# Weight conversion as a pipeline over units, and x's parts spread over the seven products, in an attention + MoE kernel

## The chip, the cores and the metric

The kernel runs on one core of a Trainium2 chip. The metric is the device time of one execution in microseconds; the comparison is between medians of several executions. The engines are named as the profile names them: PE (matmuls; PEld its weight loads), DVE (vector), ACT (scalar), POOL (GpSimd) and SP, which issues every DMA of this kernel. Each of them works through its own instructions strictly in the order of the program; instructions of different engines wait for each other by semaphores. A "DMA" is issued by SP and done by 16 shared transfer engines.

## The reference

Causal attention with a decay over 8 x 8 heads (576 positions, 64 dimensions each), and behind it a two-layer network on the 4608 tokens of 512 features. The second part is the one that the change touches:

```python
def _moe_ref(x, w_in, w_out) -> np.ndarray:
    h = x @ w_in                                   # 4608x512 @ 512x2048
    sp = np.maximum(h, 0.0) + np.log1p(np.exp(-np.abs(h)))
    g = h * erf(sp)
    return (g @ w_out).astype(np.float32)          # 4608x2048 @ 2048x512
```

The two weight matrices arrive as 64-bit floats, so the kernel has to make 32-bit floats of them itself.

## The kernel before, in words

**Two phases.** For the first 335 us the core does attention, head by head, and beside it begins to convert weights. Then comes the network ("Moe" in the code), which is all that the change moves.

**How the network is tiled.** The 4608 tokens are six blocks of 768 (`PAIR`), and the 2048 hidden features are eight units of 256. Half of the units (four, `HU`) are worked through for all six blocks, then the other half: twelve *visits* v = 0 to 11, each of four units k = 0 to 3. A *step* n = 4v + k is one unit of one visit; there are 48. Visits 0 to 5 are the first half (steps 0 to 23), visits 6 to 11 the second. A visit's partial output goes to DRAM in the first half (`part_d`) and is read back and added in the second. "A boundary" is the change from one visit to the next, step k = 3 into step k = 0.

**A step on PE.** The first product (`product`, line 149) multiplies 2x2 blocks with seven instead of eight block products; i = 0 to 6 is such a product. Every operand is carried as two parts, a rounded one and the remainder, so that each product is six matmuls of 384 columns (two along the features times three pairs of parts). x therefore stands as seven combinations, numbered r = 0 to 6, each with a rounded part and a remainder; the products use them in the order 0, 5, 1, 4, 6, 2, 3 (`XSLOT`). Only two PSUM banks (m) serve the seven products; `consume` takes a product out of its bank before a later product writes the bank again: copies `sa` and `h` on ACT (lines 162 and 167), sums `sb`, `sc` and `h` on DVE (lines 165, 170 and 173). Between the products stand the 36 matmuls of the second product (`down`, line 210, into the banks y) of the unit of two steps before; `YCUT` says after which product how many of them stand.

**Beside it, for the unit of the step before.** Four softplus and four erf on ACT (lines 177 and 180), four multiplications on DVE ("gates", line 183), four rounded copies `gh` on ACT (line 192) and four remainders `gl` on POOL (line 193), which are what `down` multiplies ("halves"). Softplus and erf need different tables in ACT: two table loads a step, at line 180 and, called for ahead of time, at line 274.

**x's parts.** `load_x` fetches the four blocks t0 to t3 of the next visit, issued at the start of k = 2. `x_sum` makes two combinations on POOL (lines 108 and 110), `late_sum` two on DVE (line 131, in place, t0 then t1); `split_x` is the rounded copy on ACT (line 117) and `rest_x` the remainder (line 123), on DVE for r = 0 and 5 and on POOL for the rest. The parts of the next visit are made in k = 3, and part 3 at the very start of its k = 0, because each part takes the place of the one that the products of k = 3 still read.

**Weight conversion.** A *piece* is 512 KB of 64-bit weights (`raw`); there are 22 in the network phase. `load` issues its DMA; `magnitude` takes the absolute value on ACT (line 372, |x|, which is in the table that erf uses and not in softplus's); `normal`, `low_bits` (two instructions) and `join` (lines 375 to 388) put a 32-bit float together on DVE; `parts` makes the rounded part on ACT (line 399) and the remainder on POOL (line 400), and for units of the second half stores both to DRAM (`wi_d`, `wo_d`; lines 402 and 403). A piece of `w_in` has one to six such pairs of parts, one of `w_out` a single one, used directly in `wo` for the first half. In the network phase all these are kept in one list, and `filler` takes the next one to three of them from it after each product, by the table `FILL`. There is one raw buffer, and the next piece is loaded at the end of `join`.

**What sets the order.** Everything is written out by hand: the program's order on each engine is the order of the calls in `step`.

## Time and profile before

| | |
|---|---|
| three runs | 1211.41, 1214.77 and 1215.17 us, median 1214.77 |
| the profiled execution | 1212.26 us, its span 1210.5 us, mean granted clock 0.967 |
| busy in the span | PE 92%, ACT 67%, DVE 59%, POOL 55% |
| attention, to step 2 | 0 to 350.7 us |
| steps 3 to 21 (conversion beside the network) | 366.8 to 767.2 us |
| steps 22 to 47 | 767.2 to 1186.5 us |
| a step that PE fills | 15.75 us |

A row of a view by stretches names the stretch in us, its length, then each engine's busy time and instructions, the granted clock of PE as a share of full speed, the DMA engines' busy share and GB/s. A row of groups has line, engine, operation, output and inputs, count, then busy us, mean ns, and the engine's idle time ahead of such instructions with what ended it. A row of waits reads "engine line <- what ended the wait: us in total, times, longest". A row of the timeline is start, duration, engine, line, operation, count and, in brackets, idle time ahead of it. A busy PE is not a PE at its peak: the half-rate clock makes it busy for longer.

### The profile page before, as it was taken

Reading aid. Unit: us, or ns where it says so; the run is one execution under the profiler, and the core shown is the slowest. Engines: PE = TensorE matmul, PEld = TensorE weight load, DVE = VectorE, ACT = ScalarE, POOL = GpSimd, SP = SyncE. Lnnn points to the kernel's source line nnn. Section 1 sums busy time; section 2 is a strip of 40 time slices with the busy share of each in tenths; the row PEclk is TensorE's granted clock in tenths of the full one; section 3 lists DMA queues with packets and bytes.
Section 4 is the critical chain, followed back from the end, with each engine's and each line's share of the span. In section 5 each row is a group of like instructions: output and inputs, shape, how many; then the busy total and the mean of one; then the engine's idle time right before and its main releaser. Section 6 shows DMA issues by size and latency. Waiting matters only on the chain. (4 is left out here: it accounts for less than half of the span.)

```text
span 1210.5 us, 21366 instructions
## 1 busy us (share of the span) xinstructions
PE 1115.7 (92%) x7384; PEld 968.0 (80%) x7384; DVE 708.3 (59%) x1696; ACT 813.2 (67%) x1746; POOL 666.6 (55%) x808
## 2 busy tenths in 40 slices
PE   8999999999997678888797989999999999999997
PEld 7888878878886567776686877989888888989896
DVE  6899989998646554555656454353444444444432
ACT  5878878878765567576767786566756656666652
POOL 5787878888815525635456436363526263553522
PEclk9999999999998798898998999999999999999999
DMA  7778777866221123251161331535040312203021
GB/s 252 239 232 262 221 234 237 290 215 201 73 90 35 53 99 119 70 170 65 61 209 35 118 135 61 214 143 209 1 156 1 111 46 68 89 28 131 9 96 70
DMA packets 74908, 155.83 MB, mean 129 GB/s; under 512 B 7472, under 2 KB 27184, under 8 KB 73776
## 3 DMA queue, kind: packets, MB, share of 16 engines
q1 hardware_dynamic: 74800, 154.47, 38.3%
q8 instruction: 59, 0.97, 0.3%
q14 instruction: 49, 0.40, 0.1%
HBM read 114.44 MB, written 39.99 MB: 128 GB/s over the span
## 5 line engine op out<-in xcount | busy, mean ns | idle before, releaser
L149 PE MATMUL m<-x,wi 128*128 128x384 f32 x2016 | 427.5, 348 | 55.6 <-DVE h L173 28.5
L149 PEld LDWEIGHTS m<-x,wi 128*128 128x128 f32 x2016 | 375.0, 194 | 95.9 <-ACT sa L162 31.8
L193 POOL TENSOR_TENSOR gl<-e,gh 128x384 fp32r<-128x384 f32 x192 | 213.3, 1142 | 393.2 <-ACT gh L192 368.4
L210 PE MATMUL y<-wo,gh 128*128 128x512 f32 x1152 | 384.0, 401 | 21.4 <-ACT wo L399 18.9
L210 PEld LDWEIGHTS y<-wo,gh 128*128 128x128 f32 x1152 | 219.5, 192 | 56.7 <-ACT wo L399 20.2
L210 PE MATMUL y<-wo,gl 128*128 128x512 f32 x576 | 231.4, 402 | 0.0
L578 POOL TENSOR_SCALAR pr<-pr,st 128x576 f32<-128x576 f32 (+4 forms) x320 | 165.1, 538 | 49.6 <-DVE st L574 29.6
L568 ACT ACTIVATE pr<-pr,st 128x576 f32<-128x576 f32 (+3 forms) x320 | 176.7, 557 | 5.0 <-DVE st L556 5.0
L556 DVE CUSTOM_DVE_ANT_0 pr<-s,c 128x576 f32<-128x576 f32 (+3 forms) x320 | 136.5, 486 | 25.5 <-PE s L540 18.2
L177 ACT ACTIVATE e<-h 128x384 f32<-128x384 f32 x192 | 92.3, 519 | 55.9 <-DVE h L173 53.3
L183 DVE TENSOR_TENSOR e<-e,h 128x384 f32<-128x384 f32 x192 | 95.4, 559 | 56.3 <-ACT e L180 56.1
L210 PEld LDWEIGHTS y<-wo,gl 128*128 128x128 f32 x576 | 111.2, 193 | 17.6
L536 PE MATMUL s<-k,q 64*128 64x320 f32 (+4 forms) x768 | 109.9, 407 | 1.9 <-DVE st L556 1.9
L599 ACT COPY pt<-t 128x512 f32<-128x512 f32 x128 | 74.0, 578 | 55.7 <-PE t L590 53.9
L165 DVE TENSOR_TENSOR sb<-m,sa 128x384 f32<-128x384 f32 x48 | 26.7, 557 | 143.8 <-PE m L149 88.5
L123 POOL TENSOR_TENSOR x<-t,x 128x768 fp32r<-128x768 f32 x55 | 108.5, 2003 | 4.1 <-ACT x L117 4.1
L590 PE MATMUL t<-ident,pr 128*128 128x128 f32 x800 | 104.7, 276 | 4.8 <-ACT pt L599 3.6
L617 PE MATMUL o<-pt,v 128*64 128x128 f32 (+1 forms) x1920 | 104.9, 263 | 3.4 <-DVE xo L626 2.3
L617 PEld LDWEIGHTS o<-pt,v 128*64 128x64 f32 x1920 | 96.0, 139 | 13.4 <-DVE st L556 4.8
L590 PEld LDWEIGHTS t<-ident,pr 128*128 128x128 f32 x800 | 87.4, 140 | 17.3 <-issue 10.8
L173 DVE TENSOR_TENSOR h<-m,sb 128x384 f32<-128x384 f32 x96 | 53.1, 553 | 82.0 <-PE m L149 81.7
L117 ACT CAST x<-t 128x768 fp32r<-128x768 f32 x77 | 61.3, 832 | 53.6 <-DVE t L131 53.4
(92 smaller groups left out, 1256.0 us busy)
## 6 DMA issues: line engine op xcount, KB each, us to landing
v<-in_vp_dram SPq DMA_DIRECT2D x32, 576.0 KB, 6.3
c<-cum_d SPq DMA_DIRECT2D x62, 288.0 KB, 5.3
t<-xt_d SPq DMA_DIRECT2D x44, 384.0 KB, 5.2
q<-in_q_dram SPq DMA_DIRECT2D x32, 320.0 KB, 3.0
k<-in_k_dram SPq DMA_DIRECT2D x32, 288.0 KB, 3.8
xt_d<-xo SPq DMA_DIRECT2D x32, 288.0 KB, 5.4
part_d<-yo SPq DMA_DIRECT2D x36, 256.0 KB, 2.1
yo<-part_d SPq DMA_DIRECT2D x36, 256.0 KB, 5.7
```

Of the source, the lines that this page charges most:

```text
L123: eng.tensor_tensor(out=x[:, 1], in0=self.src[r], in1=x[:, 0].bitcast(F32), op=ALU.subtract)
L149: nc.tensor.matmul(out=ps, lhsT=w[:, wp, ws], rhs=x[:, xp, kd], start=first and kd == 0 and j == 0, stop=kd == 1 and j == 2 and i in (1, 2 ...
L177: self.nc.scalar.activation(out=e, in_=self.h[n, q], func=AF.Softplus)
L183: self.nc.vector.tensor_mul(self.e[n, q], self.e[n, q], self.h.pop((n, q)))
L193: nc.gpsimd.tensor_tensor(out=gl, in0=e, in1=gh.bitcast(F32), op=ALU.subtract)
L210: yield nc.tensor.matmul(out=y[tb], lhsT=g[:, cs], rhs=w[:, f, wp], start=first, stop=last)
L536: nc.tensor.matmul(out=s[j][:, at:at + k1 - k0], lhsT=q[h, PAD + START[i]:PAD + END[i]], rhs=k[h, k0:k1], start=i > 0, stop=i not in (0, 3))
L556: nc.vector.tensor_tensor_reduce(out=to[:, ::-1] if j else to, in0=score, in1=decay_, scale=-0.125, scalar=BIG, op0=ALU.add, op1=ALU.min, ...
L568: nc.scalar.activation(out=seg, in_=seg, func=AF.Exp, bias=st[:, 0, j, m:m + 1], scale=-1.0, accum_out=st[:, 1, j, m:m + 1])
L578: nc.gpsimd.tensor_scalar(out=seg, in0=seg, scalar1=st[:, 2, j, m:m + 1], scalar2=1.0, op0=ALU.mult, op1=ALU.mult)
L590: nc.tensor.transpose(out=b[:, n * P:(n + 1) * P], in_=probs[t][:, at:at + P], identity=ident)
L617: nc.tensor.matmul(out=o[h, to:to + width], lhsT=v[:, ch, h], rhs=pt[:, at[j]:at[j] + width], start=n == 0, stop=n == len(parts) - 1, skip ...
```

## The change

1. **Conversion.** The list and `FILL` are gone. `late_work` gives every operation of every piece its step and its place among the seven products (`moe.work[n, i]`, run by `do`). Three pieces are converted in step 2, one in step 3, two in step 4 and one in each of steps 5 to 20, with the rounded parts and remainders of pieces 6 to 21 in the step behind. The magnitudes stand ahead of the halves in ACT's order. There are two raw buffers (and piece 2 borrows another tile), and the load of piece m + 2 stands behind the join of piece m.
2. **x's parts.** `next_x` puts `load_x` in k = 1 (visit 1: step 2), the two `x_sum` ahead of most of k = 2, and the parts of the next visit behind products 1, 4, 5 and 6 of k = 3 and product 0 of the next k = 0. The two `late_sum` and the remainder of part 0 are POOL's now; the rounded copies of parts 0, 5, 4 and 3 are DVE's.
3. **Second products.** `YCUT`: six stand behind each of products 0 to 4 and behind 6, none behind 5; before, five behind 0 to 5 and six behind 6.

The core of the diff:

```diff
-FILL = [[1, 0, 1, 1, 2, 1, 2], [1, 0, 1, 1, 1, 1, 2], [0, 0, 0, 0, 0, 1, 2]]
-YCUT = [0, 5, 10, 15, 20, 25, 30, 36]
+YCUT = [0, 6, 12, 18, 24, 30, 30, 36]
...
+    def next_x(self, v, k, i):
+
+        act, dve, pool = self.nc.scalar.copy, self.nc.vector.tensor_copy, self.nc.gpsimd
+        if k == 2 and i in ((4, 5) if v == 1 else (0, 1)):
+            self.x_sum(v, i - (4 if v == 1 else 0))
+        if k != HU - 1:
+            return
+        if i == 1:
+            self.split_x(v, 0, dve)
+            self.rest_x(v, 0, pool)
+            self.late_sum(v, 0, pool)
+        elif i == 4:
+            self.split_x(v, 5, dve)
+            self.both_x(v, 1, act, pool)
+            self.late_sum(v, 1, pool)
+        elif i == 5:
+            self.rest_x(v, 5, self.nc.vector)
+            self.both_x(v, 6, act, pool)
+        elif i == 6:
+            self.both_x(v, 4, dve, pool)
+            self.both_x(v, 2, act, pool)
...
-        if up and v and k == 0:
-            self.both_x(v, 3)
...
-        if after and k == 2:
+        if after and (n == 2 or v and k == 1):
             self.load_x(v + 1)
         for i in range(7):
             if up:
                 self.product(n, i)
                 self.consume(n, i)
+            if up and v and k == 0 and i == 0:
+                self.both_x(v, 3, self.nc.vector.tensor_copy, self.nc.gpsimd)
...
+            if after and i < 2:
+                self.next_x(v + 1, k, i)
             if gates and i == 1:
                 for q in range(4):
                     self.gate(n - 1, q)
+            if gates and i == 2:
+                self.do(n, "abs")
             if up and i == (2 if gates else 5):
                 self.nc.scalar.preload_act_table_set(SOFTPLUS)
-            if after and k == HU - 1 and i == 2:
-                self.split_x(v + 1, 0)
             if gates and i == 2:
                 for q in range(4):
                     self.halve(n - 1, q)
...
+            if after and i >= 2:
+                self.next_x(v + 1, k, i)
             for _ in range(YCUT[i + 1] - YCUT[i]):
                 next(downs, None)
-            if n >= 2:
-                self.filler(FILL[0 if n < 5 else 1 + (k == HU - 1)][i])
+            self.do(n, i)
             yield
...
-            load(m + 1)
...
+        if kind == "raw" and m == 2:
+            kind = "tt"
+        tag, bufs = {"raw": ("raw", 2), "top": ("top", 3), "tt": ("tt", 1), "hi": ("ws", 4), "lo": ("ws", 4)}[kind]
...
+    def late_work():
+
+        pieces = [(a, i) for a in range(1, HU) for i in (2, 3)] + [(a, i) for a in range(HU, NU) for i in (2, 3, 0, 1)]
...
+        for m in range(3):
+            load(m)
+        steps = {2: [0, 1, 2], 3: [3], 4: [4, 5]}
+        steps.update({n: [n + 1] for n in range(5, len(pieces) - 1)})
+        places = {1: [(3, 4, 5, 6)], 2: [(2, 3, 3, 4), (4, 5, 5, 6)], 3: [(2, 2, 3, 4), (3, 4, 4, 5), (5, 5, 6, 6)]}
+        for n, ms in steps.items():
+            for m, (a, b, c, d) in zip(ms, places[len(ms)]):
+                moe.work[n, "abs"].append(lambda m=m: magnitude(m))
+                moe.work[n, a].append(lambda m=m: normal(m))
+                moe.work[n, b].append(lambda m=m: low_bits(m))
+                moe.work[n, c].append(lambda m=m: (join(m), load({0: 3, 1: 4, 2: len(pieces)}.get(m, m + 2))))
+                i = pieces[m][1]
+                if m < 6:
+                    moe.work[n, d].append(lambda m=m: out_parts(m))
+                elif i >= 2:
+                    moe.work[n + 1, 3].append(lambda m=m: out_parts(m))
+                elif i == 0:
+                    moe.work[n + 1, 3].append(lambda m=m: quarter_parts(m, 0))
+                else:
+                    moe.work[n + 1, 1].append(lambda m=m: sums(m, 0))
+                    moe.work[n + 1, 2].append(lambda m=m: sums(m, 1))
+                    for f in range(2):
+                        moe.work[n + 1, 3 + f].append(lambda m=m, f=f: quarter_parts(m, f))
+                    for w, at in enumerate((4, 5, 5, 6)):
+                        moe.work[n + 1, at].append(lambda m=m, w=w: sum_parts(m, w))
```

Three places in the order show it; line numbers of the changed kernel are its own. The first is ACT from the copy h of step 16 on: `ltop` is a piece's magnitude, `gh` the halves of step 15, `lhi` a rounded weight part. Before:

```order
L167 COPY h16_0_8108<-m16_0_8060 128x384
L274 ACT_TABLE_LOAD
L192 CAST gh15_0_8111<-e15_0_8056 128x384
L192 CAST gh15_1_8115<-e15_1_8058 128x384
L192 CAST gh15_2_8119<-e15_2_8070 128x384
L192 CAST gh15_3_8123<-e15_3_8072 128x384
L399 CAST lhi18_8135<-ltop18_8050 128x256
L372 ACT_TABLE_LOAD
L372 ACTIVATE ltop19_8155<-lraw19_8133 128x512
L399 CAST lhi19_8204<-ltop19_8155 128x256
L399 CAST lhi19_8210<-ltop19_8155 128x256
L177 ACT_TABLE_LOAD
```

And of the change:

```order
L187 COPY h16_0_8052<-m16_0_8001 128x384
L380 ACTIVATE ltop17_8054<-lraw17_7818 128x512
L298 ACT_TABLE_LOAD
L212 CAST gh15_0_8057<-e15_0_7997 128x384
L212 CAST gh15_1_8061<-e15_1_7999 128x384
L212 CAST gh15_2_8065<-e15_2_8014 128x384
L212 CAST gh15_3_8069<-e15_3_8016 128x384
L406 CAST lhi16_8094<-ltop16_7892 128x256
L197 ACTIVATE e16_0_8143<-h16_0_8052 128x384
```

The magnitude moved ahead of the softplus table load, and the two loads around it are gone; the part that follows is of the piece before, not of the same one.

The second place is POOL at a boundary of the second half, k = 3 of step 27: `x7_r` is the remainder of part r of visit 7, `t7` a sum, `gl` the halves. Before:

```order
L193 TENSOR_TENSOR gl26_0_9784<-e26_0_9728,gh26_0_9783 128x384
L193 TENSOR_TENSOR gl26_1_9788<-e26_1_9730,gh26_1_9787 128x384
L193 TENSOR_TENSOR gl26_2_9792<-e26_2_9742,gh26_2_9791 128x384
L193 TENSOR_TENSOR gl26_3_9796<-e26_3_9744,gh26_3_9795 128x384
L123 TENSOR_TENSOR x7_1_9815<-t7_1_9587,x7_1_9815 128x768
L123 TENSOR_TENSOR x7_4_9849<-t7_4_9590,x7_4_9849 128x768
L123 TENSOR_TENSOR x7_6_9865<-t7_2_9588,x7_6_9865 128x768
L123 TENSOR_TENSOR x7_2_9868<-t7_1_9587,x7_2_9868 128x768
L123 TENSOR_TENSOR x7_3_9885<-t7_3_9589,x7_3_9885 128x768
```

And of the change:

```order
L121 TENSOR_TENSOR x7_0_9764<-t7_0_9437,x7_0_9764 128x768
L129 TENSOR_TENSOR t7_0_9437<-t7_4_9441,t7_0_9437 128x768
L213 TENSOR_TENSOR gl26_0_9788<-e26_0_9728,gh26_0_9787 128x384
L213 TENSOR_TENSOR gl26_1_9792<-e26_1_9730,gh26_1_9791 128x384
L213 TENSOR_TENSOR gl26_2_9796<-e26_2_9742,gh26_2_9795 128x384
L213 TENSOR_TENSOR gl26_3_9800<-e26_3_9744,gh26_3_9799 128x384
L121 TENSOR_TENSOR x7_1_9835<-t7_1_9438,x7_1_9835 128x768
L129 TENSOR_TENSOR t7_1_9438<-t7_1_9438,t7_0_9437 128x768
L121 TENSOR_TENSOR x7_6_9854<-t7_2_9439,x7_6_9854 128x768
L121 TENSOR_TENSOR x7_4_9865<-t7_4_9441,x7_4_9865 128x768
L121 TENSOR_TENSOR x7_2_9868<-t7_1_9438,x7_2_9868 128x768
L121 TENSOR_TENSOR x7_3_9899<-t7_3_9440,x7_3_9899 128x768
```

One remainder and one sum now stand ahead of the halves, one more sum behind them, and remainder 6 ahead of remainder 4. On DVE the same three operations are gone, and copies of parts 0, 5, 4 and 3 stand there instead; the first of them is ahead of the gates.

The third place is SP where the network's loads begin: `lraw` (and once `ltt`) is a piece of weights, `t1` a block of x. Before:

```order
L362 DMA lraw0_5695<-in_w_out_dram 128x1024
L103 DMA t1_0_5701<-xt_d_85 128x2x384
L103 DMA t1_1_5702<-xt_d_85 128x2x384
L103 DMA t1_2_5703<-xt_d_85 128x2x384
L103 DMA t1_3_5704<-xt_d_85 128x2x384
L362 DMA lraw1_5821<-in_w_out_dram 128x1024
```

And of the change:

```order
L370 DMA lraw0_5695<-in_w_out_dram 128x1024
L370 DMA lraw1_5697<-in_w_out_dram 128x1024
L370 DMA ltt2_5699<-in_w_out_dram 128x1024
L102 DMA t1_0_5705<-xt_d_85 128x2x384
L102 DMA t1_1_5706<-xt_d_85 128x2x384
L102 DMA t1_2_5707<-xt_d_85 128x2x384
L102 DMA t1_3_5708<-xt_d_85 128x2x384
L370 DMA lraw3_5820<-in_w_out_dram 128x1024
```

Three pieces are asked for ahead of x's blocks, where one was.

More of the change, by code (lines that the diff above doesn't have):

```diff
@@ L239, in finish, with do @@
             self.want_part(v, tb + 4)
-    def filler(self, count):
-        for _ in range(min(count, len(self.fill))):
-            self.fill.pop(0)()
+    def do(self, *at):
+        for f in self.work.pop(at, []):
+            f()
     def step(self, n):
@@ L348, in weight_work @@
     def weight_work(pieces, buf, cast):
-        raws, tops, work = {}, {}, []
+        raws, tops = {}, {}
         def load(m):
-            if m == len(pieces):
+            if m >= len(pieces):
                 return
@@ L426, in sums, with quarter_parts, sum_parts @@
                 nc.vector.tensor_tensor(out=t[:, at], in0=x, in1=y, op=ALU.subtract)
[L428 to L438 removed]
+        def quarter_parts(m, f):
+            in_parts(m, pieces[m][1] + f, quarter(m, f))
+        def sum_parts(m, w):
+            in_parts(m, 3 + w, tops["t"][:, w])
+        return load, magnitude, normal, low_bits, join, out_parts, quarter_parts, sums, sum_parts
     def early_buf(kind, m, shape, dt=F32):
@@ new lines, in late_work @@
+    def late_work():
+        pieces = [(a, i) for a in range(1, HU) for i in (2, 3)] + [(a, i) for a in range(HU, NU) for i in (2, 3, 0, 1)]
+        load, magnitude, normal, low_bits, join, out_parts, quarter_parts, sums, sum_parts = weight_work(
+            pieces, late_buf, nc.scalar.copy)
+        for m in range(3):
[14 more added lines that the diff above has]
+                    moe.work[n + 1, 3].append(lambda m=m: out_parts(m))
+                elif i == 0:
+                    moe.work[n + 1, 3].append(lambda m=m: quarter_parts(m, 0))
+                else:
+                    moe.work[n + 1, 1].append(lambda m=m: sums(m, 0))
[4 more added lines that the diff above has]
+                        moe.work[n + 1, at].append(lambda m=m, w=w: sum_parts(m, w))
@@ L451, in start_x @@
+    load_weight, todo = early_work()
     def start_x(j):
@@ L725, in attention_moe @@
     moe.ps_y = ctx.enter_context(tc.tile_pool(name="ps_y", bufs=1, space=PSUM))
[L726 to L728 removed]
+    late_work()
     last = HU * NPAIR
@@ L741, in attention_moe @@
     moe.reload = reload
-    total = len(moe.fill)
     for n in range(2, moe.n + 2):
-        assert len(moe.fill) <= max(total - 8 * (n - 2), total - 24) and (n < last - HU or not moe.fill)
         for _ in moe.step(n):
             pass
-    assert not moe.fill
+    assert not moe.work
 def kernel(q, k, v, f, moe_w_in, moe_w_out):
```

78 lines of the change are left out of this document (28 added, 50 removed).

## The prediction, made before the changed kernel had run

> **What bounds the kernel now.** I read the busy time by stretches first, cut where step n's first product starts on PE. Steps 3 to 21 lie in 366.83:767.24, steps 22 to 47 behind it; 847.81:912.65 is one undisturbed visit (four steps) of the second half, and the four rows ahead of the totals are single steps (3, 4, 16 and 17).
>
> ```profile
> core 0: us, PE busy (x) PEld busy (x) DVE busy (x) ACT busy (x) POOL busy (x), PEclk, DMA share, GB/s
> 366.83:393.14 26.31, 19.00 (x79) 15.69 (x78) 18.76 (x21) 14.39 (x24) 13.61 (x9) 0.87 0.06 21
> 393.14:424.05 30.91, 19.65 (x78) 16.62 (x79) 15.88 (x18) 16.70 (x27) 17.04 (x11) 0.78 0.15 51
> 650.23:677.80 27.57, 20.31 (x79) 17.71 (x79) 14.63 (x20) 16.88 (x26) 15.37 (x12) 0.81 0.20 67
> 677.80:693.55 15.75, 15.75 (x79) 14.19 (x78) 7.54 (x16) 12.58 (x24) 6.79 (x8) 1.00 0.38 128
> 366.83:767.24 400.41, 332.51 (x1484) 287.93 (x1482) 216.04 (x306) 266.50 (x447) 194.72 (x153) 0.91 0.28 95
> 767.24:1186.54 419.30, 410.35 (x2024) 366.95 (x2023) 183.77 (x291) 261.15 (x461) 193.98 (x146) 1.00 0.26 91
> 847.81:912.65 64.84, 63.34 (x313) 56.59 (x312) 29.34 (x46) 40.35 (x71) 31.00 (x24) 1.00 0.22 74
> ```
>
> A step that PE fills at full clock takes 15.75 us (step 17). Nineteen of them are 299.3, and steps 3 to 21 took 400.4: **101.1 us too many**, 67.9 of it PE idle (400.4 - 332.5) and some 33 slower matmuls (332.5 - 299.3), which go with a granted clock of 0.91 there and 1.00 behind it. The 26 later steps took 419.3 where 26 x 15.75 = 409.5 would do: 9.8 us, lost 1.8 at a time (64.84 - 63.0) at the change from one visit to the next. No other engine is near full in either stretch. So an edit gains by removing waits in steps 3 to 21, and can gain hardly anything elsewhere. Next, what PE waited for there:
>
> ```profile
> PE m L149 <- ACT sa L162: 25.6, 10, 5.7
> PE m L149 <- DVE h L173: 19.5, 10, 4.1
> PE y L210 <- ACT wo L399: 18.9, 3, 10.3
> ```
>
> These are evacuations that come late because ACT and DVE, which work in order, are held by the weight conversion. Groups of ACT in steps 3 to 21, then two loads in step 16 and PE's wait behind them:
>
> ```profile
> L177 ACT ACT_TABLE_LOAD x15 | 19.2, 1283 | 0.3
> L372 ACT ACT_TABLE_LOAD x14 | 18.0, 1283 | 14.3 <-DMA lraw<-in_w_in_dram 8.2 <-DMA lraw<-in_w_out_dram 5.9
> L372 ACT ACTIVATE ltop<-lraw 128x512 f32<-128x512 f32 x21 | 14.0, 665 | 8.6 <-DMA lraw<-in_w_in_dram 4.8 <-DMA lraw<-in_w_out_dram 3.6
> 657.61 1.28 ACT L372 ACT_TABLE_LOAD   x1
> 661.17 1.28 ACT L177 ACT_TABLE_LOAD   x1
> 663.82 2.29 PE L149 MATMUL m<-x,wi 128*128 128x384 f32 x6 [3.85 <-ACT sa L162]
> ```
>
> The magnitude (L372) stands after the softplus table was called for: it loads a table, waits for its piece, and the softplus loads its own back. That is 37 us of ACT time in loads and 23 in waits for pieces. The pieces are late because of the queue that issues them (SP's own waits; microseconds, times, longest), not because of the transfer:
>
> ```profile
> SPq L362 <- DVE ltop L387: 164.7, 18, 25.4
> lraw<-in_w_out_dram SPq DMA_DIRECT2D x14, 512.0 KB, 3.8
> ```
>
> **The change, part by part.** *Table loads and pieces.* Thirty table loads go (15 at L372, 15 at L177; the order of the changed kernel has none there), and a load is issued after the join two pieces earlier, about one step ahead of its use, against 3.8 us to land. Nothing is added on ACT: the 22 magnitudes stay, 0.67 each, now ahead of the halves' table load. The casts of parts move to the next step or a later place. So I take the waits for pieces and tables as gone; their cover, if a load is late after all, is the step of 15.75 minus 3.8. For a table switch the Trainium skill ("ScalarE: Activation LUTs", What ACT_TABLE_LOAD costs) gives about 2.66 us, half of it a drain after the 1283 ns; here softplus starts 10 ns after the load, so this case shows the 1283 alone. By that page of the Trainium skill the thirty would be 80 us of ACT, by the row they are 38.5.
>
> *What comes in its place: x's parts.* Two sums and one remainder per visit move from DVE to POOL, four copies from ACT to DVE, and POOL works during the gates of step k = 3. Rows of the second half, k = 3 starting at 847.81 (DVE, POOL, ACT, PE):
>
> ```profile
> 851.33 0.56 DVE L165 TENSOR_TENSOR sb<-m,sa 128x384 f32<-128x384 f32 x1 [4.15 <-PE m L149]
> 852.31 1.96 DVE L183 TENSOR_TENSOR e<-e,h 128x384 f32<-128x384 f32 x4 [0.42 <-ACT e L180]
> 856.19 0.95 DVE L123 TENSOR_TENSOR x<-t,x 128x768 fp32r<-128x768 f32 x1
> 857.24 1.60 DVE L131 TENSOR_TENSOR t<-t,t 128x768 f32<-128x768 f32 x1
> 864.23 2.58 DVE L131 TENSOR_TENSOR t<-t,t 128x768 f32<-128x768 f32 x1 [2.24 <-POOL x L123]
> 866.74 0.54 DVE L173 TENSOR_TENSOR h<-m,sb 128x384 f32<-128x384 f32 x1
> 840.12 3.95 POOL L193 TENSOR_TENSOR gl<-e,gh 128x384 fp32r<-128x384 f32 x4 [11.48 <-ACT gh L192]
> 856.61 5.78 POOL L193 TENSOR_TENSOR gl<-e,gh 128x384 fp32r<-128x384 f32 x4 [8.79 <-ACT gh L192]
> 862.36 1.84 POOL L123 TENSOR_TENSOR x<-t,x 128x768 fp32r<-128x768 f32 x1
> 866.90 1.57 ACT L117 CAST x<-t 128x768 fp32r<-128x768 f32 x2 [5.73 <-DVE t L131]
> 868.38 0.93 ACT L177 ACTIVATE e<-h 128x384 f32<-128x384 f32 x2
> 869.21 0.46 ACT L162 COPY sa<-m 128x384 f32<-128x384 f32 x1
> 867.42 1.29 PE L149 MATMUL m<-x,wi 128*128 128x384 f32 x6 [1.50 <-DVE h L173]
> ```
>
> Two things. The 1.8 us come from the sum L131: DVE's last evacuation (866.74) stands behind it. That queueing goes, since the sum is POOL's now. But DVE and POOL take turns: the same 768 elements take DVE 0.95 alone and 2.58 beside POOL, and POOL's four halves 5.78 instead of 3.95, as if each operation waited for the other engine's to end. The Trainium skill ("SBUF — State Buffer", Who interferes with whom) says that the pair of ports is an exclusive lock against DVE operations with two SBUF inputs and two-port copies; the rows agree, and it speaks against moving work between these two. Prices of what is moved, all from other places of the trace:
>
> ```profile
> L399 DVE CAST wi<-top 128x256 fp32r<-128x256 f32 x12 | 3.4, 313 | 0.2
> L399 DVE CAST wo<-top 128x512 fp32r<-128x512 f32 x2 | 1.0, 522 | 0.1
> L108 POOL TENSOR_TENSOR t<-t,t 128x768 f32<-128x768 f32 x6 | 11.1, 1854 | 0.9 <-DMA t<-xt_d 0.9
> L400 POOL TENSOR_TENSOR llo<-ltop,lhi 128x512 fp32r<-128x512 f32 x8 | 10.5, 1313 | 21.6 <-ACT lhi L399 21.6
> 359.17 0.69 DVE L375 SCALAR_TENSOR_TENSOR ltop<-ltop,lraw 128x512 f32<-128x512 f32 x1 [1.96 <-ACT ltop L372]
> 360.24 0.42 DVE L380 TENSOR_SCALAR lraw<-ltop 128x512 int32<-128x512 int32 x1
> ```
>
> A DVE copy of 768 elements isn't in the trace: between 0.52 (512 elements) and 0.95 (the two-input operation of 768); I take 0.73, the line through 313 and 522.
>
> *A boundary without conversion (second half).* PE's products now start 2.45 us apart (2.22 before plus one second product of 0.23). The copy of x's part 0 follows the evacuation sb (851.33, 3.5 us into the step, now 0.23 later), so it ends 3.5 + 0.23 + 0.56 + 0.73 = 5.0 us into k = 3. From there POOL has remainder 0 (1.84), sum 0 (1.85), four halves (3.95), remainder 1 (1.84) and sum 1 (1.85), 11.3 us; in turns with it DVE has three gates (0.47 each, by the four in 1.96), the copy and the remainder of part 5 (0.73 + 0.95): 3.1. Sum 1 ends at 19.4. ACT's copy of part 2 waits for it (0.8), then two softplus (0.93) and the copy sa (0.46) to 21.6, and PE wants sa for the third product of k = 0 at 15.75 + 4.9 = 20.65: 1.0 late. Then four remainders and two copies (7.4 + 1.5) keep POOL busy to 28.3, that is 12.5 into k = 0, beside that step's gates, behind which DVE's evacuation sc stands; PE wants it for the sixth product at 5 x 2.45 + 1.0 = 13.2. That is 0 to 1.5 more. I take **1.4 us** a boundary (0.3 to 2.5) for 1.8 now.
>
> *A boundary with a conversion piece (first half).* To these turns come POOL's remainder of a piece (1.31) and DVE's four operations (0.69 + 0.42, and two of the same size as the first: 2.5), ahead of evacuations h that PE's next banks wait for: 1.4 + 3.8 = 5.2. I take **5 us** (1.5 to 8) at four of them, steps 7/8, 11/12, 15/16 and 19/20.
>
> *The start.* Three pieces are loaded at once, ahead of x's four tiles. Step 2 starts at 350.7; its magnitude, and PE's wait in step 3:
>
> ```profile
> 358.47 0.66 ACT L372 ACTIVATE ltop<-lraw 128x512 f32<-128x512 f32 x1 [2.09 <-DMA lraw<-in_w_out_dram]
> 373.50 0.79 PE L210 MATMUL y<-wo,gh 128*128 128x512 f32 x1 [4.78 <-ACT wo L399]
> ```
>
> With two more transfers of 512 KB ahead of it (an estimate: half of the 3.8 for each) the third magnitude ends near 358.5 + 3.8 + 0.7 = 363. A table load, the first half, POOL's four halves, a sum and the first weight remainder follow: 1.3 + 0.5 + 3.95 + 1.85 + 1.3, so 372. PE wants that remainder at 350.7 + 15.75 + 1.3 = 367.8, and the second comes 3.2 behind the first: 7 us of waiting in step 3. In step 4 PE wants the fourth piece's remainder, the last POOL operation of step 3. That step's x chain starts near 378 and has 14.4 + 3.8 us to sum 1, three remainders and this one (6.8): 403 if every turn is taken, against 391 wanted; I take 9. With 4 for the clock that such gaps cost (0.78 and 0.87 above) and 2 for steps 5 and 6 I put **22 us** on steps 3 to 6 (12 to 34); before, steps 3 and 4 alone lost 25.7 (26.31 + 30.91 - 31.5).
>
> *Elsewhere.* The six parts of a piece in a k = 1 step go through four buffers whose stores have to land; I allow 0.5 us four times. Two us are for lost clock at the boundaries. Seven groups of second products instead of eight cost PE nothing (their sum is the same 36).
>
> *Sum.* Steps 3 to 21: 22 + 4 x 5 + 2 + 2 = 46 instead of 101.1, 55 gained. Six boundaries of the second half: 6 x 0.4 = 2.4. Together 57.5. The profiled run took 1212.3 (span 1210.5 and 1.8 around it): 1154.8. The median shown is 2.5 above that run, so 1157.3 by it; I say **1156 us**.
>
> **Rivals.** *The pair of ports never binds* (conversion and x fit into the waits that DVE and POOL have, both below 60% busy in 366.83:767.24): boundaries of 1 us, start 18, so 26 left: 75 gained, and 5 in the second half, 1135; with the start at 12, 1129. Against it: eight POOL operations of 1.85 in a step and a half.
>
> *Slower than before.* The place is again the boundary, now all ten. If each of the four gates of k = 3 and of k = 0 waits for a whole 1.85 operation, as the sum at 864.23 did, that is 8 x 1.85 = 14.8 less some 4 of slack, 11 us each: 22 + 4 + 110 = 136 against the 111 lost now, 1240 us. It decides from 8.5 us a boundary on. For it: the 2.58. Against it: in this trace POOL is idle when the gates run, and a gate needs only one of POOL's gaps.
>
> *The pieces are still late.* If stores ahead of a load in SP's queue hold it, only the table loads' 38.5 us are gained: 1176. Against it: in the order there is a whole step between issue and use.
>
> *No effect*, ACT off the path: 1215. The 3.85 us of PE behind sa speak against it.
>
> **How the numbers follow.** Forecast 0.62, free ports 0.20, late pieces 0.10, slower 0.05, no effect 0.03. The bounds together: best 12 + 4 x 1.5 + 2 = 20 left in steps 3 to 21 and 1.5 gained at each later boundary, 90 in all, 1125; worst 34 + 4 x 8 + 4 = 70 left and 0.7 lost at each later one, 27 in all, 1188. The range is **1120 to 1188**. A difference under 0.3% (3.6 us) can't be told from none here. Faster 0.92, same 0.03, slower 0.05.
>
> **What would show it.** Right: no table load at the magnitude's or the softplus's line; SP's wait for the join off the path; steps away from boundaries at 15.75; PE's waits at a boundary ended by sa, sc or h, with POOL's remainders up to 12 us into k = 0; step 4 waiting for a remainder wo of POOL. Wrong: boundaries of the first half at 1 us or over 8; step 3 or 4 without a wait; an ACT wait for a piece over 1 us; second-half visits longer than 64.84.

## The result and the profile after

The changed kernel takes **1158.35 us** (median of four runs, 1155.07 to 1160.88) where the kernel before takes 1214.97 beside it (1211.41 to 1216.09): a ratio of **0.9537, 95% interval 0.9504 to 0.9571**. The forecast was 1156 in a range of 1120 to 1188. The profiled run took 1156.83, its span 1155.0.

The view by stretches of the changed kernel, cut at the steps' starts as before (length, then busy time and instructions of PE, PEld, DVE, ACT and POOL, granted clock, DMA). In order: steps 3, 4, 5, 6, 7 (k = 3), 8 (k = 0), 10 (k = 2), 12 (k = 0), then steps 3 to 21, steps 22 to 47, and a visit of the second half.

```profile
366.51:391.71 25.20, 19.51 (x79) 16.49 (x78) 16.44 (x18) 11.36 (x20) 20.60 (x14) 0.80 0.04 16
391.71:419.07 27.36, 18.81 (x79) 16.21 (x78) 15.98 (x20) 11.70 (x21) 18.11 (x12) 0.81 0.12 39
419.07:436.87 17.80, 16.20 (x80) 13.98 (x78) 11.30 (x17) 12.30 (x23) 8.52 (x7) 1.00 0.51 177
436.87:452.51 15.64, 15.64 (x80) 14.07 (x79) 9.64 (x16) 9.92 (x18) 9.09 (x7) 1.00 0.27 85
452.51:469.38 16.87, 15.80 (x79) 13.87 (x77) 13.11 (x14) 10.65 (x18) 12.12 (x9) 1.00 0.19 68
469.38:489.31 19.93, 16.58 (x78) 13.99 (x79) 18.65 (x17) 11.14 (x21) 18.01 (x11) 1.00 0.15 49
504.95:521.89 16.94, 15.91 (x80) 13.98 (x78) 9.57 (x15) 12.25 (x24) 11.12 (x11) 1.00 0.53 179
538.76:558.37 19.61, 17.59 (x78) 15.45 (x79) 18.32 (x17) 11.34 (x21) 17.98 (x11) 0.91 0.13 43
366.51:713.25 346.74, 311.97 (x1483) 273.35 (x1482) 251.43 (x306) 211.45 (x389) 242.07 (x167) 0.96 0.31 107
713.25:1131.38 418.13, 407.34 (x2024) 363.93 (x2023) 238.00 (x297) 248.22 (x443) 236.00 (x168) 1.00 0.26 91
808.63:873.43 64.80, 62.85 (x314) 56.15 (x313) 38.71 (x48) 37.82 (x67) 37.66 (x27) 1.00 0.22 74
```

Steps 3 to 21 took 346.7 us instead of 400.4: 53.7 gained there. Steps 22 to 47 gained 1.2 (419.3 to 418.1). Together 54.8 of the 55.4 between the two profiled runs (1212.26 and 1156.83), so next to nothing happened elsewhere. Of the 53.7, 33.1 are less idle time of PE (67.9 to 34.8) and 20.5 are less busy time for the same matmuls (332.5 to 312.0); most of that goes with the granted clock, 0.96 there instead of 0.91. A step that PE fills is 15.64 us now, 0.11 shorter than before. Nineteen of them are 297.2, so 49.6 us are still lost in steps 3 to 21. PE's waits there, and then in steps 22 to 47 (us in total, times, longest):

```profile
PE m L169 <- DVE h L193: 12.6, 8, 2.0
PE y L230 <- POOL wo L407: 12.4, 4, 5.9
PE m L169 <- ACT sa L182: 3.7, 3, 1.8
PE y L230 <- ACT wo L406: 3.4, 2, 2.7
PE m L169 <- DVE sc L190: 2.4, 2, 1.2
...
PE m L169 <- DVE sc L190: 10.7, 6, 2.0
```

The 25.6 us behind sa have become 3.7, the 18.9 behind the rounded part wo 3.4, the 19.5 behind h 12.6. PE waits 12.4 us for POOL's remainder wo (11.6 in steps 3 and 4, the rest in step 5), 2.4 before, and in the second half the wait at a boundary is for sc instead of h. Groups of the changed kernel: ACT's table loads in the network, the magnitude, and DVE's gates:

```profile
L298 ACT ACT_TABLE_LOAD x48 | 61.6, 1283 | 0.8
L200 ACT ACT_TABLE_LOAD x48 | 61.6, 1283 | 0.9
L380 ACT ACTIVATE ltop<-lraw 128x512 f32<-128x512 f32 x21 | 14.0, 672 | 0.7 <-DMA lraw<-in_w_out_dram 0.6
L203 DVE TENSOR_TENSOR e<-e,h 128x384 f32<-128x384 f32 x192 | 185.9, 1028 | 33.1 <-ACT e L200 28.2 <-POOL x L121 4.6
```

The thirty table loads around the magnitudes are gone, and ACT waits 0.7 us for pieces. The price stands in the last row: a gate takes 1028 ns, since POOL works beside it, and took 559 in the same group of the kernel before:

```profile
L183 DVE TENSOR_TENSOR e<-e,h 128x384 f32<-128x384 f32 x192 | 95.4, 559 | 56.3 <-ACT e L180 56.1
```

Last, a boundary of the second half. Step 32 (k = 0) starts at 873.43; POOL, DVE and PE:

```profile
873.58 2.44 POOL L129 TENSOR_TENSOR t<-t,t 128x768 f32<-128x768 f32 x1
875.99 8.22 POOL L121 TENSOR_TENSOR x<-t,x 128x768 fp32r<-128x768 f32 x4
884.28 4.74 POOL L213 TENSOR_TENSOR gl<-e,gh 128x384 fp32r<-128x384 f32 x4
...
880.88 6.32 DVE L203 TENSOR_TENSOR e<-e,h 128x384 f32<-128x384 f32 x4 [1.84 <-ACT e L200]
887.12 0.55 DVE L190 TENSOR_TENSOR sc<-m,sb 128x384 f32<-128x384 f32 x1
...
887.72 2.35 PE L169 MATMUL m<-x,wi 128*128 128x384 f32 x12 [1.94 <-DVE sc L190]
```

The four gates take 6.32 us (1.96 for four in the profile before, with POOL idle): the first two run beside the last two of POOL's four remainders, the other two beside its halves gl. Then sc stands behind them in DVE's order, and PE waits 1.94 for sc.

### The profile page after: what moved, and what is told of

It reads as the page before. It is cut to its first block, busy times and chain, and to the rows that moved or that the text cites. A ratio compares the mean times of both kernels' runs of the same rounds, so it can differ in the third digit from the quotient of the medians.

```text
span 1155.0 us, 21292 instructions
## 1 busy us (share of the span) xinstructions
PE 1092.3 (95%) x7384; PEld 951.1 (82%) x7384; DVE 800.1 (69%) x1707; ACT 745.7 (65%) x1672; POOL 753.5 (65%) x841
## 4 chain that ended last, share of the span: by engine, by line
PE 64%; POOL 12%; DVE 10%; ACT 6%; issue 4%; DMA 3%; SPq 0%; DVEq 0%; POOLq 0%; ACTq 0%
PE y L230 21%; PE m L169 20%; PE s L585 8%; PE o L666 8%; PE t L639 7%; POOL gl L213 4%; DVE e L203 3%; POOL x L121 3%; POOL t L129 3%; ACT e L200 2%; ACT e L197 2%; ACT L200 1%; DMA wi_d<-lhi 1%; DMA xt_d<-xo 1%; DVE ltop L395 1%
## 5 line engine op out<-in xcount | busy, mean ns | idle before, releaser
L169 PE MATMUL m<-x,wi 128*128 128x384 f32 x2016 | 404.7, 339 | 29.7 <-DVE sc L190 13.1
L169 PEld LDWEIGHTS m<-x,wi 128*128 128x128 f32 x2016 | 361.3, 190 | 63.0 <-DVE h L193 16.9
L230 PE MATMUL y<-wo,gh 128*128 128x512 f32 x1152 | 363.4, 396 | 16.0 <-POOL wo L407 12.4
L213 POOL TENSOR_TENSOR gl<-e,gh 128x384 fp32r<-128x384 f32 x192 | 221.5, 1183 | 236.4 <-ACT gh L212 209.5
L230 PEld LDWEIGHTS y<-wo,gh 128*128 128x128 f32 x1152 | 214.6, 190 | 46.8 <-POOL wo L407 14.1
L203 DVE TENSOR_TENSOR e<-e,h 128x384 f32<-128x384 f32 x192 | 185.9, 1028 | 33.1 <-ACT e L200 28.2
L121 POOL TENSOR_TENSOR x<-t,x 128x768 fp32r<-128x768 f32 x66 | 135.9, 2076 | 65.1 <-DVE x L116 65.1
L605 DVE CUSTOM_DVE_ANT_0 pr<-s,c 128x576 f32<-128x576 f32 (+3 forms) x320 | 136.5, 486 | 28.3 <-PE s L589 19.5
L185 DVE TENSOR_TENSOR sb<-m,sa 128x384 f32<-128x384 f32 x48 | 26.7, 555 | 146.7 <-PE m L169 112.7
L648 ACT COPY pt<-t 128x512 f32<-128x512 f32 x128 | 73.9, 577 | 55.5 <-PE t L639 53.7
L212 ACT CAST gh<-e 128x384 fp32r<-128x384 f32 x192 | 88.9, 511 | 29.6 <-DVE e L203 28.7
L639 PEld LDWEIGHTS t<-ident,pr 128*128 128x128 f32 x800 | 87.4, 141 | 15.2 <-issue 11.6
L585 PEld LDWEIGHTS s<-k,q 64*128 64x128 f32 x768 | 73.1, 188 | 32.1 <-issue 17.6
```

The source lines that it names most:

```text
L121: eng.tensor_tensor(out=x[:, 1], in0=self.src[r], in1=x[:, 0].bitcast(F32), op=ALU.subtract)
L169: nc.tensor.matmul(out=ps, lhsT=w[:, wp, ws], rhs=x[:, xp, kd], start=first and kd == 0 and j == 0, stop=kd == 1 and j == 2 and i in (1, 2 ...
L203: self.nc.vector.tensor_mul(self.e[n, q], self.e[n, q], self.h.pop((n, q)))
L213: nc.gpsimd.tensor_tensor(out=gl, in0=e, in1=gh.bitcast(F32), op=ALU.subtract)
L230: yield nc.tensor.matmul(out=y[tb], lhsT=g[:, cs], rhs=w[:, f, wp], start=first, stop=last)
L585: nc.tensor.matmul(out=s[j][:, at:at + k1 - k0], lhsT=q[h, PAD + START[i]:PAD + END[i]], rhs=k[h, k0:k1], start=i > 0, stop=i not in (0, 3))
```

## The experiments

Each is an edit of the kernel before or of the changed kernel. The times are medians beside the kernel before on the same chip (1213.15 to 1215.31 there), the ratio is to that.

**1. The second products alone** (kernel before, only `YCUT` changed).

```diff
-YCUT = [0, 5, 10, 15, 20, 25, 30, 36]
+YCUT = [0, 6, 12, 18, 24, 30, 30, 36]
```

> The kernel before with only the new places of the second products. The prediction put this part at nothing: 1213 to 1216 us, a filled step at 15.75. Rival: a filled step of the changed kernel takes 15.64 in the trace, so that the pair of switches between first and second products that is saved costs PE 0.11 us; then steps that PE fills take 15.64 and the kernel gains 3 to 5 us (26 to 48 steps), 1210 to 1212.

1216.45 us, ratio 1.0017 (1.0000 to 1.0034): nothing gained. One filled step and one visit of the second half of this kernel:

```profile
847.88:863.51 15.63, 15.63 (x79) 14.06 (x78) 8.24 (x11) 11.67 (x19) 6.92 (x6) 1.00 0.01 1
863.51:928.30 64.79, 62.79 (x313) 56.14 (x312) 29.12 (x46) 40.36 (x71) 31.19 (x24) 1.00 0.23 74
```

This edit is what makes the filled step 0.11 shorter, but the visit stays at 64.8 (64.84 before): its k = 0 step went to 17.87, since PE arrives earlier at the same evacuation h and waits longer, up to 2.00 instead of 1.50.

**2. The loads alone** (kernel before, a second raw buffer, each load two pieces ahead; order and table loads as before).

```diff
-            load(m + 1)
+            load(m + ahead)
...
-        tag, bufs = {"raw": ("raw", 1), "top": ("top", 2), "tt": ("tt", 1), "hi": ("ws", 4), "lo": ("ws", 4)}[kind]
+        tag, bufs = {"raw": ("raw", 2), "top": ("top", 2), "tt": ("tt", 1), "hi": ("ws", 4), "lo": ("ws", 4)}[kind]
```

> The kernel before with two raw buffers and each piece of the network phase asked for at the join two pieces earlier; nothing else moved. If the waits of ACT for pieces (23 us in steps 3 to 21) were on PE's path, 10 to 23 us are gained: 1192 to 1205. If the loss was in what stands where in the engines' order, and the waits for pieces only let ACT stand where it would have stood for the next join anyway, less than 5: 1210 to 1216.

1189.69 us, ratio 0.9797 (0.9775 to 0.9819). Steps 3 to 21 took 378.4, 22.0 less than before. That stretch, and PE's two longest waits in it:

```profile
365.70:744.09 378.39, 322.67 (x1484) 280.48 (x1482) 218.87 (x305) 266.25 (x446) 196.43 (x153) 0.94 0.30 99
PE m L149 <- ACT sa L162: 20.3, 7, 4.4
PE m L149 <- DVE h L173: 19.4, 10, 4.5
```

Early pieces alone are worth some 23 us in the order of the kernel before. Of the 22.0, 12.2 are idle time of PE (55.7 after 67.9) and 9.8 busy time, at a granted clock of 0.94 after 0.91. The wait for wo fell from 18.9 to 12.4; the waits for sa and h are still 20.3 of 25.6 and 19.4 of 19.5. Those had been late for another reason too.

**3. The table loads back** (changed kernel, the magnitude behind the halves, so in softplus's time; 135 table loads instead of 97).

```diff
-            if gates and i == 2:
-                self.do(n, "abs")
...
                 for q in range(4):
                     self.halve(n - 1, q)
+                self.do(n, "abs")
```

> The changed kernel with the 19 groups of magnitudes behind the halves again, so that 38 table loads (48.8 us of ACT at 1.283) come back. If ACT's table loads were what the steps lost, 38 to 49 us come back: 1196 to 1207. If ACT has room for them (211 us busy in the 346.7 us of steps 3 to 21 of the changed kernel, so 11.1 + 2.6 = 13.7 in a step of 15.64), under 10: 1158 to 1168.

1185.37 us, ratio 0.9766 (0.9741 to 0.9791): 27 us over the change, between the two outcomes expected; 24.2 of them in steps 3 to 21 (370.9). PE's waits there, DVE's longest, and ACT in one step:

```profile
PE m L169 <- DVE h L193: 35.2, 19, 3.1
PE m L169 <- ACT sa L182: 6.5, 4, 3.4
...
DVE ltop L382 <- ACT ltop L379: 48.9, 17, 5.6
...
448.41 1.28 ACT L296 ACT_TABLE_LOAD   x1
449.70 1.76 ACT L212 CAST gh<-e 128x384 fp32r<-128x384 f32 x4
451.47 1.28 ACT L379 ACT_TABLE_LOAD   x1
452.77 0.67 ACT L379 ACTIVATE ltop<-lraw 128x512 f32<-128x512 f32 x1
```

The loss isn't where a full ACT would put it: sa waits 6.5. DVE's `normal` stands 48.9 us waiting for a magnitude that comes two table loads and four halves late (some 4.3 us by these rows, 2.6 of it the loads), the evacuation h stands behind it in DVE's order, and PE waits 35.2 us for h. The edit moves the magnitude behind the halves as well, so it doesn't part the loads from the place. This kernel has more table loads than the one before (135 to 127) and is still 28 us faster, so the time doesn't follow the sum of the loads on ACT; it follows what stands behind the late magnitude.

**4. x's parts as before** (changed kernel; sums, copies and remainders on the engines and at the places of the kernel before).

```diff
+        if up and v and k == 0:
+            self.both_x(v, 3, act, pool)
...
-        if after and (n == 2 or v and k == 1):
+        if after and k == 2:
...
-                self.next_x(v + 1, k, i)
...
+                if i == 3:
+                    self.rest_x(v + 1, 0, dve)
+                    self.late_sum(v + 1, 0, dve)
+                    self.both_x(v + 1, 1, act, pool)
+                elif i == 4:
+                    self.both_x(v + 1, 5, act, dve)
+                elif i == 5:
+                    self.late_sum(v + 1, 1, dve)
+                    self.both_x(v + 1, 4, act, pool)
+                elif i == 6:
+                    self.both_x(v + 1, 6, act, pool)
+                    self.both_x(v + 1, 2, act, pool)
...
```

> The changed kernel with x's parts made as before the change: load at k = 2, sums 0 and 1 and remainder 0 on DVE, all rounded copies on ACT, at their old places. By the prediction's sum the move of x's parts is worth little: boundaries of the second half go back from 2.2 to 1.8 us, those of the first half stay near 5: 1150 to 1165. Rival: the spread of x's parts is what shortened the first half's boundaries (8 to 12 us there before): 4 to 7 us each come back, 1175 to 1190.

1159.39 us, ratio 0.9536 (0.9510 to 0.9562): the time of the change. The group of its gates:

```profile
L203 DVE TENSOR_TENSOR e<-e,h 128x384 f32<-128x384 f32 x192 | 105.2, 608 | 35.0 <-ACT e L200 34.6 <-POOL t L107 0.2
```

And PE's only wait in its second half:

```profile
PE m L169 <- DVE h L193: 12.0, 6, 2.0
```

The gates are quick again and the boundary waits for h again, 2.0 instead of 1.94 for sc. In the first half the k = 3 steps take 19.1 and the k = 0 steps 17.5, where the change has 16.9 and 19.6: 36.6 and 36.5 for the pair. Two other steps of its profile differ and nearly cancel: step 4 is 4.2 shorter than in that of the change and step 14 is 4.4 longer. The second part of the change moves waits from one step to the next and from h to sc, and gains nothing.

**5. Gates split** (changed kernel; at k = 0 the gates 2 and 3 and their halves behind the evacuation sc).

```diff
+            late = (2, 3) if up and v and k == 0 else ()
...
+            if gates and i == 3:
+                for q in late:
+                    self.gate(n - 1, q)
+                    self.halve(n - 1, q)
```

> The changed kernel with two of the four gates of each step k = 0 (visits 1 to 11), and their halves, behind the evacuation sc instead of ahead of it. If sc is late only because it stands behind four gates that take turns with POOL's remainders, the wait of 1.94 us at each boundary of the second half goes and a step k = 0 takes 15.6 to 16.2 there instead of 17.87: 10 to 13 us gained, 1145 to 1149. If another product is late there as well (a remainder of x not made, h behind the late gates), the wait only changes its name: 17 or more, 1154 to 1159.

1155.14 us, ratio 0.9513 (0.9497 to 0.9529). PE's only wait in the second half:

```profile
PE m L169 <- DVE h L193: 5.0, 6, 0.9
```

The wait for sc is gone, so it was the gates ahead of it; the next evacuation h now stands behind the two moved gates. A step k = 0 of the second half takes 16.9 to 17.1, so neither expectation is met in full. Steps 22 to 47 took 413.5, 4.6 less. The time fell by 3 us only, and the interval overlaps that of the change; in its profile step 14 was 3.9 longer than in that of the change (see the point "elsewhere" below).

**6. The start reordered** (changed kernel; the two sums for visit 1 behind step 2, and in step 3 the weight's remainder ahead of x's remainders 4 and 2).

```diff
-        if k == 2 and i in ((4, 5) if v == 1 else (0, 1)):
-            self.x_sum(v, i - (4 if v == 1 else 0))
+        if k == 2 and i in (0, 1) and v != 1:
+            self.x_sum(v, i)
...
+            if n == 3 and i == 6:
+                self.do(n, i)
...
+            if n == 2 and i == 6:
+                self.x_sum(1, 0)
+                self.x_sum(1, 1)
```

> The changed kernel with POOL's sums for visit 1 behind the three weight remainders of step 2, and the fourth piece's remainder ahead of x's remainders 4 and 2 in step 3. By the prediction's account of the start PE's waits for wo (12.4 us in four waits of steps 3 to 5) shrink by 5 to 9 us: 1149 to 1153. Rival: x's chain, now later by the same operations, holds PE instead: 1156 to 1160.

1150.90 us, ratio 0.9484 (0.9455 to 0.9514). The stretches of steps 3 and 4:

```profile
361.24:384.71 23.47, 18.13 (x80) 14.80 (x78) 18.17 (x18) 11.46 (x20) 22.67 (x16) 0.93 0.03 13
384.71:407.12 22.41, 19.50 (x78) 16.41 (x79) 18.03 (x20) 11.72 (x21) 16.99 (x11) 0.77 0.16 48
```

And PE's wait for POOL's remainder in steps 3 to 21:

```profile
PE y L230 <- POOL wo L412: 4.3, 3, 2.9
```

6.7 us less in these two steps (45.9 after 52.6), 8.1 less waiting for wo, and a median 7.5 lower: POOL's order did set the start. The two steps still lose 14.6 together.

**7. Conversion behind the evacuations** (changed kernel; in k = 3 steps `low_bits` and `join` behind the last product, where DVE's evacuations have been done).

```diff
-            for m, (a, b, c, d) in zip(ms, places[len(ms)]):
+            for m, (a, b, c, d) in zip(ms, [(3, 6, 6, 6)] if n > 4 and n % HU == HU - 1 else places[len(ms)]):
```

> The changed kernel with low bits and join of a piece behind all evacuations in the steps k = 3 with conversion (7, 11, 15, 19). If PE's waits for h at the first half's boundaries (12.6 us in eight waits) come from these operations standing ahead of h on DVE, k = 3 goes from 16.9 to 15.7 and the boundary from 5.4 to 3 or 4 us: 5 to 10 us gained, 1149 to 1154. If the time is POOL's and DVE's turns whatever their order, k = 0 grows by what k = 3 loses: 1156 to 1160.

1154.56 us, ratio 0.9522 (0.9489 to 0.9556), not to be told from the change. The k = 3 steps of the first half are filled (15.64), and the k = 0 steps went from 19.6 to between 21.0 and 22.5. PE's longest sum of waits in steps 3 to 21 is now

```profile
PE m L169 <- ACT sa L182: 12.6, 7, 2.8
```

against 3.7. The 1.2 us of a k = 3 step moved into the next one: the work of DVE and POOL for the boundary is the same, and only the wait that ends last is another.

**8. Remainders halved** (changed kernel; each of POOL's remainders of x as two operations of 384 elements).

```diff
+        if v and eng is self.nc.gpsimd:
+            for kd in range(2):
+                eng.tensor_tensor(out=x[:, 1, kd], in0=self.src[r][:, kd], in1=x[:, 0, kd].bitcast(F32), op=ALU.subtract)
+            return
```

> The changed kernel with each of POOL's remainders of x (768 elements, 1.85 us) made as two of 384. If DVE and POOL take turns operation by operation, each gate of k = 0 waits for at most half as long, sc comes 2 to 3 us earlier, and the 1.94 us at a boundary of the second half shrinks to under 1: a step k = 0 at 16.0 to 16.9, 1147 to 1153. If they share the port's rate, or if POOL's total decides, nothing changes or the added instructions cost: 17.87 or more, 1157 to 1163.

1153.13 us, ratio 0.9498 (0.9478 to 0.9517). PE's waits in the second half:

```profile
PE m L173 <- DVE sc L194: 5.8, 6, 1.0
PE m L173 <- ACT sa L186: 3.7, 6, 0.6
```

And DVE in step 32, whose k = 0 starts at 870.46:

```profile
878.84 5.29 DVE L207 TENSOR_TENSOR e<-e,h 128x384 f32<-128x384 f32 x4 [2.19 <-ACT e L204]
884.05 0.54 DVE L194 TENSOR_TENSOR sc<-m,sb 128x384 f32<-128x384 f32 x1
```

Beside POOL operations of half the size the four gates take 5.29 instead of 6.32: a gate waits for the POOL operation under way to end, and for one at a time. But they start 8.4 us into the step instead of 7.5, behind a sum 1 that ends 19.2 us into k = 3 instead of 18.2, so sc is done only 0.1 earlier (14.1 us into the step for 14.2), where 2 to 3 were expected. The wait for sc is shorter (5.8 for 10.7) because PE, held 0.6 by sa first, arrives later. A k = 0 step still takes 17.77. The time's interval overlaps that of the change.

**9. Loads one piece ahead** (changed kernel; from piece 6 on, each piece's load at the join of the one before it, not two before).

```diff
-load({0: 3, 1: 4, 2: len(pieces)}.get(m, m + 2))
+load({0: 3, 1: 4, 2: len(pieces), 3: 5, 4: len(pieces)}.get(m, m + 1))
```

> The changed kernel with pieces 7 to 21 asked for at the join of the piece before, not two before. In the new order that join stands behind product 5 of one step and the magnitude behind product 2 of the next, four products or 9.8 us, against 3.8 us to land: nothing changes, 1155 to 1161, if the new place of the magnitude and not the second piece ahead made the pieces timely. If two ahead is what made them timely (stores ahead of a load in SP's queue hold it), ACT waits for pieces come back and 8 us or more are lost.

1155.99 us, ratio 0.9514 (0.9495 to 0.9534): as the change. With the magnitudes at their new place, a load at the join of the piece before is early enough; the second piece in flight adds nothing to the time. Steps 3 to 21 took 349.9.

**10. Boundary and start together** (changed kernel with experiment 6; at k = 0 gate 2 behind sc and gate 3 behind the h that follows; x's part 2 made at k = 0 behind the erfs, so that ACT's copy no longer stands ahead of sa).

```diff
-            self.both_x(v, 2, act, pool)
...
+                if up and v and k == 0:
+                    self.both_x(v, 2, self.nc.scalar.copy, self.nc.gpsimd)
...
+            late = {3: 2, 4: 3} if up and v and k == 0 else {}
...
+            if gates and i in late:
+                self.gate(n - 1, late[i])
+                self.halve(n - 1, late[i])
```

> The changed kernel with the reordered start of the earlier run, gate 2 of k = 0 behind sc and gate 3 behind the h that follows it (their halves with them), and part 2 of x made in k = 0 behind the erfs, so that ACT's softplus and sa no longer stand behind it. If the waits left at a boundary are evacuations that stand behind turns, k = 0 of the second half takes 15.6 to 16.2, boundaries of the first half lose 1 to 3 us, and with the start 18 to 25 us are gained: 1133 to 1140. If POOL's chain itself ends too late for a product, k = 0 stays at 16.9 and the gain is the start's and the gates' alone: 1145 to 1149.

**1133.47 us, ratio 0.9328 (0.9309 to 0.9347)**, about 25 under the change. Steps 22 to 47 of it:

```profile
702.98:1108.39 405.41, 405.41 (x2024) 364.37 (x2023) 230.15 (x297) 249.04 (x443) 237.34 (x168) 1.00 0.28 94
```

PE is busy for all of the 405.41: no boundary of the second half is left. That is 12.7 of the gain; the start gave 6.5 (23.32 and 22.72 for steps 3 and 4). The boundaries of the first half didn't shrink to the 1 to 3 us expected: three of them still lose 5.2 and the first 4.3, with waits for h at each. In its profile step 3 also began 5.3 earlier than in that of the change (361.2 to 366.5), in attention that no edit here touches: and such a shift is seen without cause elsewhere (366.8 in the kernel before, 363.4 in experiment 1, where that phase is the same). So some 18 of the 25 (12.7 and 5.0 in steps 3 to 21, the start in it) are the edit's by its steps, and the rest isn't settled.

**11. The same with the conversion of experiment 7.**

```diff
+            for m, (a, b, c, d) in zip(ms, [(3, 6, 6, 6)] if n > 4 and n % HU == HU - 1 else places[len(ms)]):
```

> The run before with low bits and join behind all evacuations in the steps k = 3 with conversion. That edit alone moved the loss from k = 3 into k = 0 by way of sa (12.6 us of waits). With sa freed from part 2 it should now keep what it wins in k = 3 (1.2 us, four times): 3 to 5 us below the run before. If k = 0 grows again, the same time.

1139.32 us, ratio 0.9375 (0.9351 to 0.9399): 6 worse than without it. The first half's k = 3 steps are filled again, its k = 0 steps take 21.0, and PE's largest wait in steps 3 to 21 is for DVE again:

```profile
PE m L168 <- DVE sb L184: 11.1, 4, 2.8
```

A gain of 3 to 5 was expected. The four boundaries together are only 1.6 longer than in experiment 10 (146.7 us for the eight steps, 145.1 there); what the rest of the 6 is isn't settled.

**12. And with the halved remainders of experiment 8** (to the kernel of 11).

```diff
+        if v and eng is self.nc.gpsimd:
+            for kd in range(2):
+                eng.tensor_tensor(out=x[:, 1, kd], in0=self.src[r][:, kd], in1=x[:, 0, kd].bitcast(F32), op=ALU.subtract)
+            return
```

> The run before with POOL's remainders of x halved as well: shorter turns, 1 to 4 us less if gates still wait for whole remainders in front of an evacuation that PE wants; 0 to 3 us more if nothing waits there any longer and only POOL's added instructions count.

**1132.80 us, ratio 0.9325 (0.9306 to 0.9345)**: the same as 10 within the intervals, by another way. Its steps 3 to 21:

```profile
362.89:699.97 337.08, 313.33 (x1483) 273.95 (x1482) 241.39 (x306) 211.95 (x389) 252.05 (x197) 0.96 0.33 110
```

337.1 against 346.7 of the change, with filled k = 3 steps and k = 0 steps of 19.0 to 20.2. PE's wait at these boundaries is then for POOL's remainders themselves (6.8 us in eight waits) more than for an evacuation. In the median, smaller POOL operations pay back what the conversion's place lost, but not more; the halved remainders on the kernel of 10, without that place, weren't run.

## Why the prediction held, point by point

*What bounds the kernel: right.* All but 1.7 us of the gain lies in steps 3 to 21, and the mechanism is the one named, an in-order ACT and DVE held by the conversion. Experiments 1 and 4 take out the other two parts of the change: neither gains by itself. But the step that counted the thirty table loads as 37 us of ACT time doesn't say how a late magnitude costs. In the order of the kernel before, PE waits longest for ACT's own sa; in that of the change, by experiment 3, it is for DVE, whose evacuation h is queued behind `normal`, and sa is held far less. Early pieces were worth 22 us of steps 3 to 21 in the old order (experiment 2), and the magnitude's place 24 in the new one (experiment 3). The two don't add up as parts of the 53.7: with loads only one piece ahead the new order keeps 50.5 of them (experiment 9), so it makes the pieces timely by itself. How the rest divides between the new places of DVE's conversion and of the parts wasn't run.

*Start: right, one wait smaller than forecast.* 22 us were put on steps 3 to 6, and 23.4 are measured (25.20, 27.36, 17.80 and 15.64, less four times 15.64). The waits for wo are 4.33 and 1.36 in step 3 and 2.67 and 5.88 in step 4, 14.2 in all where 7 and 9 were said; the 2.67 are for ACT's rounded part, which the sum didn't have. The slower clock (0.80 and 0.81) made up for it: PE was busy 19.51 and 18.81 in steps 3 and 4 instead of 15.64, 7.0 us where 4 were allowed. The 2.2 us lost in step 5 fit the 2 said.

*Boundaries of the first half: right.* 5 us were said for each. The four k = 3 steps lose 1.2 to 1.4 and the four k = 0 steps 4.0 to 4.3: 5.2 to 5.7. The bank's wait is ended by h, as said (1.1 to 1.2 us at the first product of k = 0, which the cut puts into k = 3, and 2.0 further on); then sc adds 1.2 in steps 8 and 20, and in steps 12 and 16 a granted clock of 0.91 makes PE busy for 17.6 us instead of 16.6.

*Boundaries of the second half: the term with the wrong sign.* A gain of 0.4 each was put in the sum, 1.4 instead of 1.8 us. Measured is 2.23 (17.87 less 15.64) at five of the six, and 1.54 in step 24. The step that failed is the order of the two waits. It had sa 1.0 late, behind sum 1 at 19.4 us into k = 3, and sc "0 to 1.5 more", of which hardly any was taken. Sum 1 ended at 18.2 (876.02 less 857.79), so sa came in time; and sc was late by all of 1.94, because the gates took 1.58 each beside POOL's work instead of some 0.5. The mechanism stood in the text, at 0.4 us of the 1.4. A smaller price was off too: the DVE copy of 768 elements, put at 0.73, took 0.55 alone and up to 2.2 beside POOL. The boundary isn't even always the same. In the profiles of experiments 6, 7 and 9, whose edits don't touch the second half, a k = 0 step takes 17.2 (sum 1 at 18.7, and one gate of 0.55), 17.9, or 19.4 (the wait of 17.9 with a granted clock of 0.91). That visits are no longer than before all the same (64.80 to 64.84) comes from the next point.

*"Seven groups of second products instead of eight cost PE nothing": wrong.* By `YCUT` there are six groups instead of seven, and the new cut saves PE 0.11 us a step, 15.64 for 15.75, as experiment 1 shows. But the saved time reached the end only where nothing was waited for; with 4 x 0.11 = 0.4 less per visit and 0.4 more at its boundary it is the reason for the unchanged 64.8. That two misjudged terms nearly cancel there is luck.

*Elsewhere: right place, too small.* Two us were allowed for parts that wait for buffers whose stores have to land, and 2 for lost clock at the boundaries. Measured are 4.5 us in steps 10, 14 and 18 (16.94, 17.66 and 16.87 for 15.64). The lost clock is the 1.0 us each of steps 12 and 16, so about 2 as allowed; it is in the boundaries' 21.6 already. ACT's last two casts of step 14 and the copy sa behind them:

```profile
576.38 0.41 ACT L406 CAST lhi<-ltt 128x256 fp32r<-128x256 f32 x1 [2.73 <-DMA wi_d<-lhi]
578.35 0.41 ACT L406 CAST lhi<-ltt 128x256 fp32r<-128x256 f32 x1 [1.56 <-DMA wi_d<-lhi]
...
580.28 0.47 ACT L182 COPY sa<-m 128x384 f32<-128x384 f32 x1
...
580.80 1.31 PE L169 MATMUL m<-x,wi 128*128 128x384 f32 x6 [1.75 <-ACT sa L182]
```

The casts of the k = 1 step are pushed into k = 2, ahead of sa; here and in step 18 by stores that haven't landed, in step 10 by POOL's remainders (0.81 us before the last cast but one). Step 14 is also the step that varies most: 17.7 us here and 21.6 in experiment 5, whose edit isn't in it. A fifth buffer wasn't tried.

*The sum.* Left over in steps 3 to 21: 23.4 + 21.6 + 4.5 = 49.5 over steps of 15.64, which is 47.4 over the 15.75 that the forecast counts from, where 46 were said; gained 53.7 for 55, and 1.2 for 2.4 behind. With the two profiled runs 55.4 for 57.5.

*The rivals.* Free ports (boundaries of 1 us) is out by 5.2 to 5.7 at each and by the gates' 1028 ns. Slower by whole POOL operations ahead of every gate is out in its size, not in its kind: each gate does wait for one, but 1.1 at a time (1.58 less 0.47) at k = 0, and the slack takes most of it. Late pieces is out by ACT's 0.7 us of waiting, and no effect by the result.

## What to carry to other kernels

Look for the operation that stands ahead of an evacuation in an in-order queue and depends on another engine: here a late magnitude on ACT cost the time through DVE, and having that one short operation ahead of a table switch and four halves was worth 24 us. Work moved between two engines that take turns, or made later or in smaller pieces on them, only changed which evacuation is late (experiments 4, 7 and 8), while putting the evacuations ahead of the contended work, with one copy moved off ACT's way, removed the wait in the second half (experiment 10). A saving on the bounding engine is worth nothing at a place where that engine then waits longer for the same thing (experiment 1).
